# Who begins the first loads: two keys of the first step on ScalarE's queue, queries and a weight piece ahead of the next keys

## The chip, the cores and the metric

The kernel runs on one core of one Trainium2 chip. The metric is the device time of one execution in microseconds; lower is better.

## The reference

A delta-rule attention is followed by a two-layer network with a hard-swish.

```python
# q, k, v: (4, 8, 768, 48); beta: (4, 8, 768)
k_n = k / (np.linalg.norm(k, axis=-1, keepdims=True) + 1e-06)
for t in range(768):
    y[:, :, t] = einsum('bhd,bhde->bhe', q[:, :, t], state)
    v_old = einsum('bhde,bhd->bhe', state, k_n[:, :, t])
    state += beta[:, :, t] * outer(k_n[:, :, t], v[:, :, t] - v_old)
x = y.transpose(0, 2, 1, 3).reshape(3072, 384)
h = x @ w_in                       # (384, 2048)
g = h * clip(h + 3, 0, 6) / 6
out = g @ w_out                    # (2048, 384)
```

q, k, v and beta come as float32, the two weights as float64.

## The kernel before, in words

The 768 positions are taken in 24 steps of 32. In one step the 4 batches times 32 positions fill the 128 partitions, and the 8 heads lie side by side. A step t goes through these stages:

- `load_k` (L161) and `load_q` (L173) load its keys and queries, one DMA of 48 KB for each of the 4 batches, issued by SP (L168 and L180). `load_v` does the same for the values (L193).
- `norms` (L399): ScalarE squares the keys (L407), VectorE sums them (L413), ScalarE takes the root (L417), VectorE makes the inverse norm in four small instructions on the tiles `nt` and `inv` (L420, L422, L426, L431).
- `prep` (L505): GpSimd scales the keys into `kb` (L510); TensorE transposes keys and then queries (L524), and ScalarE copies each result out of PSUM into `KQ` (L532); TensorE forms the scores (L547), and VectorE masks them into `X` or `L` and `LB` (L558).
- The inverse of the lower triangle, for step 0 in `product` (L569): small products on TensorE (`pi`, L596) between VectorE transposes (L612, L626, L631 and so on) and copies by ScalarE (L624, L643). Steps 1 to 4 are inverted together by a chain on VectorE (`halves_of`), the later ones by fours.
- `chain` (state, output) on TensorE, and, two steps to a block, the two layers (`up`, `down` and their forms with fewer products), which are most of TensorE's time.

The weights arrive as float64 in 16 pieces of 768 KB, issued by SP in `load_w` (L331). Each is turned into float32 on the chip: four ScalarE activations over the piece (`scales`, L356), and three VectorE passes (`convert`, L378, L383, L389). The pieces w0 to w7 are of `w_in`. Beta comes in four loads of 24 KB, issued by ScalarE (`betas`, L1383), and is turned by VectorE (L255) into `beta_tok`. Constants are made in `settings`, among them `places` (L273), which the activations at L356 read. ScalarE's activation table is loaded at the head of the program (L201), followed by a copy of one column (L202).

The order of the opening is written out by hand in the string `ORDER`. Each word advances a generator by one step: `k` issues one of the 4 loads of a step's keys, `q` one of the queries, `w` one weight piece, `B` one beta load, `n0` one stage of the norms of step 0, `p0` one stage of its `prep`, `x0` one of its inverse, `a` one activation of `scales`, `c` one pass of `convert`, `z` and `s` settings, `m` masks. Every engine runs its own instructions in the order in which the words emit them.

The framework gives the loads of SP and ScalarE, in the order of the program, one of eight completion counters in turn. A load is held on its issuing engine until the load that had the same counter before it, eight loads earlier, has landed.

Of the kernel before, what the change touches and what calls it, by code (L numbers as in the profile page):

```python
# [19 lines left out]


ORDER = """
k*2 B*3 k*2 n0 k*2 z B s*2 n0*6 k*2 q*2 n1 q n1 q w k p0 z*3 k n1*2 k*2 n1*2 z p0*2 s k p0*3 a k a
m0 a n2 m1 p0 x0*2 w q x0 n1 x0*3 c*2 n2 a k s p1*2 a s*2 k q s*2 x0 n2 k*2 c x0 n2 x0 w q a*4 q p1
n2 k*2 a x0 m2 p1 c*2 p1 n2*3 b1 q b0 s p1 x0 q w x0 n2 q*2 c*3 x0 n4 k p1 k p2*2 x0*2 a*2 c a*2 q*3
a*2 w v p3*2 q x0 q n4 p2*2 c p2 v c n4*2 a*3 z v n4 c a m3 v c p2 n4*2 q p2 k c b2 h0 c h0 w a*2 h0
p4*2 a*2 m4 p3 q*4 h0 q k w p4*2 c*5 v*2 p3 k p3*3 k*2 p4*2 v*2 p4 m6 k a w a w i1*3 k i1*7 a i1*2 a
i1*2 v i1*2 k b3 k y0 c y0*3 ua*2 ra*2 i1*3 w v ga v a*3 i1*2 ua i1 h1 i1 q w ua ra ua i1 ra*2 ga i1
k ua a*2 ra ga i1 ga ua ra ua ra i1 ga i1*4 ua ga n5 x1*2 k x1 c a ra v a*2 ga x2 k*2 ga*2 ua*2 x1
ra*2 x1*2 ua h1*2 n5 k ga c ra ga*2 h1 c y1*2 ua ra w ga ua ra x2 n5 ga y1*2 ua ra ga h1 v*3 n5*2 k  # L30
y1*2 ua a ra x2 ub*2 a n5 rb*2 h1 x3 ga c*2 v W a h2 y2 gb ub rb gb x2 gb ub*2 n5*2 b4 rb n5 x2*2 h2
gb rb gb m5 a n5*2 ub rb gb v c q*2 v q*5 n5 ub n5 rb gb h2 y2 c h2 q ub y2*2 rb ub p5 b5 h2 rb gb*2
a*2 x3 p5 ub y2*2 k p5*2 h2 rb h3 p5 gb h3 ub*2 q rb gb rb gb ub a x3 p6 v c x4 x3 rb gb ub p7 rb gb
y3 c*2 v c p7*2 y3 v p7*2 b6 x3 q x3 ub h3 a p6*2 c p5*2 rb gb k m7 w p6 h3 u p6 k*2 q*3 a*2 y3 a p6
c y3 v y3*2 u n9 v k q a c a c*2 u*2 ru gu w k a*2 c a*2 x4 c*2 ru p7 a gu k u a*2 p7 p6 m8 u*3 a k
u*2 k h3 w ru*2 a*2 gu*2 x4 c*2 x4 k c*2 a p8 k a*2 u ru k h3 u*2 h4 ru a b8 gu k gu y4 p8*3 u h4
k*2 c q k*9 q u p8*2 k ru k*2 gu k c n9 q u q*2 p8 k*2 b7 n9*2 x4 i2 u x4 q i2*2 q ub ru gu u rb gb
i2*2 h4*2 u*2 i2 ru i2*6 y4 i2 gu i2*7 u i2 ru gu i2 u*3 ru i2*4 gu ru i2*2 v i2 c gu u*3 a u ru c
i2 u*2 i2 gu i2*3 q i2*5 y4 n9 i2 e*2 n9*2 i2*4 q i2 y4 e n9 u ru i2*3 u h4 i2 ru*2 gu h4 u n9 i2*2
u i2 e i2*6 y4 u k n9*3 u gu i2 y4 n9 i2 p9 q i2*2 gu  # L40
"""


# [1 line left out]
def kernel(  # L45
# [21 lines left out]
    nc = tc.nc  # L67
# [27 lines left out]
    def rows(b):  # L95
        return slice(C * b, C * b + C)
# [34 lines left out]
    def tokens(ap, b, t):  # L131
        return ap[b, :, t * C : (t + 1) * C, :].rearrange("h t d -> t h d")
# [25 lines left out]
            past.add(("read", key))  # L158
            reads.setdefault(key, len(reads))

    def load_k(t, eng=nc.sync):  # L161

        g, i = group(t)
        if g not in kfs:
            needs(*(("kb", first(g - 2) + j) for j in range(size(g - 2) if g >= 2 else 0)))
            kfs[g] = stage.tile([P, GS, H, D], FP32, name="kf", bufs=2)
        for b in range(B):
            eng.dma_start(out=kfs[g][rows(b), i], in_=tokens(k, b, t))  # L168
            if b == B - 1:
                past.add(("k", t))  # L170
            yield

    def load_q(t, eng=nc.sync):  # L173
        if t < N:
            if t >= NQB:
                needs(("qT", t - NQB))
            elif t:
                needs(*pad(t))
            for b in range(B):
                eng.dma_start(out=qbufs[t % NQB][rows(b), :, 0:D], in_=tokens(q, b, t))  # L180
                if b == B - 1:
                    past.add(("q", t))
                yield
# [14 lines left out]
    halves = const.tile([128, 2], FP32, name="halves")  # L198
    nc.vector.memset(halves[:], 0.5)
    half = halves[:, 1:2]  # L200
    nc.scalar.preload_act_table(ACTF.Sqrt)  # L201
    nc.scalar.activation(out=half, in_=halves[:, 0:1], func=ACTF.Copy)  # L202

    spare = const.tile([128, 3, NFC // 2 * DM // 2], FP32, name="spare")
    assert S <= spare.shape[2]
# [44 lines left out]
    def settings():  # L250

        nc.vector.memset(tiny, 1e-30)
        pads(nc.vector, kbufs[0], qbufs[0])
        yield
        nc.vector.transpose(out=beta_tok[:].rearrange("p n h -> p (n h)"), in_=beta_hm)  # L255
        past.add("beta")
        yield
        nc.vector.tensor_reduce(
            out=eye[:], in_=ident[:].rearrange("p (b c) -> p c b", b=B), axis=AX.X, op=ALU.add
        )  # L260
        nc.vector.tensor_reduce(
            out=blocks[:], in_=eye[:].rearrange("p (n c) -> p n c", c=G), axis=AX.X, op=ALU.add
        )
        past.add("blocks")
        yield
        nc.vector.tensor_reduce(
            out=corner[:], in_=ident[:].rearrange("p (b c) -> p c b", b=B)[:, C // 2 : C],
            axis=AX.X, op=ALU.add,
        )
        past.add("corner")  # L270
        yield
        for i, (_, _, value) in enumerate(powers):
            nc.vector.memset(places[:, i : i + 1], value)  # L273
        past.add("places")
        yield
        nc.vector.memset(parity[:], 0.0)
        for b in range(B):
            for j, value in enumerate((-1.0, 1.0)):
                nc.vector.memset(parity[rows(b), b % 2, j : j + 1], value)
        past.add("parity")  # L280
        yield
# [5 lines left out]
    def more_settings():  # L287
        for t in range(NBKB):
            pads(nc.gpsimd, bkbufs[t], *(x[t] for x in (kbufs, qbufs) if 0 < t < len(x)))
            past.add(f"pad{t}")  # L290
            yield
            if t == 1:
                nc.gpsimd.memset(state[:], 0.0)
                past.add(("state", -1))
                yield
# [49 lines left out]
    def scales():  # L345

        needs("places", "beta")
        for i in range(NW):
            if weights[i][1].dtype == FP32:
                continue  # L350
            if i >= 2:
                needs(("w", i - 2))
            needs(("raw", i))
            d, z = raws[i], like(es[i % 2], i)
            for n, (func, scale, _) in enumerate(powers):
                nc.scalar.activation(  # L356
                    out=z, in_=z if n else d.bitcast(I16)[:, :, :, 3], func=func,
                    bias=places[:, n : n + 1], scale=scale,
                )
                if n == 0:  # L360
                    past.add(("seen", i, 0))
                if n == len(powers) - 1:
                    past.add(("scale", i))
                yield
# [1001 lines left out]
    def pieces():  # L1366
        for i in range(NW):
            load_w(i)
            yield

    def queries():
        for t in range(N):
            for _ in load_q(t):
                yield

    def keys():
        for t in range(first(4) + GS):
            for _ in load_k(t):
                yield

    def betas():
        for b in range(B):
            nc.scalar.dma_start(out=beta_hm[C * b : C * b + H, :], in_=beta[b])  # L1383
            yield

    def values():
        for t in range(N):
            for _ in load_v(t):
                yield

    def early_norms(t):
# [4 lines left out]
    g_all = mlp.tile([128, NFC, TB], FP32, name="g", bufs=1)  # L1396
    rest = chained(convert(), quarters())
    gens.update(
        a=scales(), c=rest, w=pieces(), q=queries(), v=values(), B=betas(), k=keys(), z=settings(), s=more_settings(),
        ua=up(0, 0), ub=up(0, 1), u=mlp_units(),  # L1400
    )
    makers = {
# [4 lines left out]
    def behind_tensor(ins):  # L1407
        last = next(
            i for i in reversed(nc.cur_bb.bb.instructions) if i.engine == mybir.EngineType.PE
        )  # L1410
        tc.add_manual_dep(
            ins, last.name,
            mybir.DependencyInfo(mybir.DependencyClass.Sync, mybir.DependencyReason.DATA),
            reason="held back",
        )

    def do(word):
        if word in ("K", "Q", "V", "W"):
            n = len(nc.cur_bb.bb.instructions)
            next(gens[word.lower()])  # L1420
            (new,) = nc.cur_bb.bb.instructions[n:]
            behind_tensor(new)
        elif word in gens:
            next(gens[word])
        elif word[0] == "r":
            relus[word[1]].pop(0)()
        elif word[0] == "g":
            pending[word[1]].pop(0)()
        elif word == "e":
            evicts.pop(0)()  # L1430
        elif word[0] == "i":
            next(inverse_of(int(word[1:])), None)
        else:
            name, t = word[0], int(word[1:])
            if name == "p" and t >= LS + LE:
                next(prep_of(t), None)
            else:
                key = (name, t) if name in "hp" else ("early", name, t)
                next(made(key, lambda: makers[name](t)), None)
# [111 lines left out]
```

## Time and profile before

| | us |
|---|---|
| median of 3 runs | 667.3 |
| the runs | 667.3, 666.17, 667.43 |
| profiled execution | 665.93 |
| its span (first to last instruction) | 664.1 |
| TensorE matmul busy | 636.2 (96%) |
| VectorE busy | 487.1 (73%) |
| ScalarE busy | 272.1 (41%) |
| GpSimd busy | 203.5 (31%) |
| first key load issued (SP) | 0.80 |
| first Square on ScalarE (L407) | 4.78 |
| first weight piece issued (SP) | 6.75 |
| first L356 on ScalarE | 12.33 |

In the profile PE is TensorE, PEld its weight loads, DVE VectorE, ACT ScalarE, POOL GpSimd and SP SyncE; SPq and ACTq are issues of DMAs by the queues of SP and ScalarE. Line numbers are those of the kernel before; in the changed kernel the lines from L207 to L1383 stand five lower (L407 is L412), and the key loads are at L170. The granted clock is TensorE's, as a share of full speed.

### The profile page before, as it was taken

How to read it: one execution, taken by the hardware profiler on the slowest of the kernel's cores; microseconds unless marked ns; L12 is line 12 of the kernel's file. 1: busy time of each engine (PE TensorE's matmuls, PEld its weight loads, DVE VectorE, ACT ScalarE, POOL GpSimd, SP SyncE). 2: the span in 40 equal slices, each digit the busy share in tenths (PEclk: the TensorE clock that was granted, in tenths of full speed). 3: DMA queues.
4: the chain of work that ended last, by engine and by line, in shares of the span. 5: the costliest groups of instructions: out<-in, count | busy, mean ns of one | idle time of the engine just before them, and what ended most of it. 6: DMA issues, size and time to landing. Idle time of an engine off the chain costs nothing.

```text
span 664.1 us, 26330 instructions
## 1 busy us (share of the span) xinstructions
PE 636.2 (96%) x11544; PEld 568.1 (86%) x11544; DVE 487.1 (73%) x1146; ACT 272.1 (41%) x532; POOL 203.5 (31%) x320
## 2 busy tenths in 40 slices
PE   2769999999999999999999999999999999999997
PEld 1658987776789989989989999999999999999997
DVE  4899867898555697657979748989658998456353
ACT  5897679331233143142144244244244144153350
POOL 6531112003511320562254354064052241331430
PEclk9659999999999999999999999999999999999999
DMA  7897246212140030041030030020020020000000
GB/s 175 206 236 197 76 98 161 49 28 41 23 83 8 10 66 3 2 85 27 2 74 3 2 74 3 3 61 2 3 50 2 2 50 1 23 19 2 25 1 25
DMA packets 88499, 33.27 MB, mean 50 GB/s; under 512 B 80160, under 2 KB 83232, under 8 KB 88384
## 3 DMA queue, kind: packets, MB, share of 16 engines
q1 hardware_dynamic: 88128, 31.29, 20.9%
q8 instruction: 91, 1.49, 0.9%
q10 hardware_dynamic: 256, 0.30, 0.2%
q14 instruction: 24, 0.20, 0.1%
HBM read 26.84 MB, written 4.72 MB: 48 GB/s over the span
## 4 chain that ended last, share of the span: by engine, by line
PE 90%; DVE 3%; DMA 2%; SPq 2%; ACT 1%; issue 1%; POOL 0%; ACTq 0%; DVEq 0%; POOLq 0%
PE po L1218 28%; PE ph L1066 20%; PE ph L994 16%; PE po L1154 6%; PE ks L806 3%; PE pt L524 3%; PE su L938 3%; PE pz L827 3%; PE py L827 3%; PE sc L547 3%; PE yt L873 1%; DMA spare<-in_moe_w_in_dram 1%; PE pi L684 1%; DMA w_out<-in_moe_w_in_dram 1%; SPq L168 1%
## 5 line engine op out<-in xcount | busy, mean ns | idle before, releaser
L1066 PE MATMUL ph<-xT,w_in 128*128 128x128 f32 (+1 forms) x560 | 121.4, 321 | 0.7 <-ACT KQ L532 0.5
L994 PE MATMUL ph<-xT,w_in 128*128 128x256 f32 (+1 forms) x576 | 117.1, 353 | 0.9 <-ACT xT L877 0.6
L1218 PE MATMUL po<-w_out,g 128*128 128x192 f32 x640 | 110.6, 326 | 0.0
L994 PEld LDWEIGHTS ph<-xT,w_in 128*128 128x128 f32 x576 | 95.2, 194 | 13.9 <-ACT xT L877 1.0
L1218 PEld LDWEIGHTS po<-w_out,g 128*128 128x128 f32 x640 | 104.6, 190 | 0.5
L1066 PEld LDWEIGHTS ph<-xT,w_in 128*128 128x128 f32 x560 | 91.1, 191 | 5.9 <-ACT KQ L532 0.7
L1030 POOL TENSOR_TENSOR g<-g 128x256 f32<-128x256 f32 x112 | 67.9, 608 | 83.2 <-ACT g L1080 78.8
L1218 PE MATMUL po<-spare,g 128*128 128x192 f32 x480 | 86.7, 332 | 0.0
L1218 PEld LDWEIGHTS po<-spare,g 128*128 128x128 f32 x480 | 77.2, 190 | 1.8
L1001 ACT ACTIVATE g<-ph,halves 128x256 f32<-128x256 f32 (+1 forms) x96 | 41.0, 436 | 74.2 <-PE ph L994 74.2
L1228 POOL TENSOR_TENSOR o<-o,u 128x192 f32<-128x192 f32 x18 | 13.2, 731 | 175.8 <-ACT o L1225 97.2
L1080 ACT ACTIVATE g<-ph 128x512 f32<-128x512 f32 x56 | 33.4, 597 | 81.8 <-PE ph L1066 81.8
L1204 DVE TENSOR_TENSOR g<-g 128x512 f32<-128x512 f32 x80 | 55.5, 715 | 5.6 <-PE po L1218 5.6
L759 DVE TENSOR_TENSOR pr<-A 128x30 f32<-128x30 f32 (+9 forms) x150 | 57.5, 383 | 2.7
L764 DVE TENSOR_TENSOR A<-A,pr 128x30 f32<-128x30 f32 (+9 forms) x150 | 55.7, 371 | 3.7
L1004 DVE SCALAR_TENSOR_TENSOR g<-g,ph 128x256 f32<-128x256 f32 (+1 forms) x96 | 34.7, 371 | 29.4 <-ACT g L1001 29.0
L356 ACT ACTIVATE spare<-spare,places 128x768 uint16<-128x768 uint16 (+1 forms) x56 | 52.6, 944 | 2.8 <-DMA kf<-in_k_dram 1.7
L1093 DVE TENSOR_TENSOR g<-ph,g 128x256 f32<-128x256 f32 x56 | 23.5, 420 | 38.5 <-PE ph L1066 30.9
L1225 ACT ACTIVATE o<-po 128x192 f32<-128x192 f32 x40 | 13.2, 330 | 83.2 <-PE po L1218 79.6
L1154 PE MATMUL po<-w_out,g 128*128 128x384 f32 x128 | 45.2, 491 | 0.0
L1107 DVE SCALAR_TENSOR_TENSOR g<-o,g 128x512 f32<-128x512 f32 x56 | 40.7, 726 | 5.9 <-ACT o L1104 5.9
L1104 ACT ACTIVATE o<-g,halves 128x512 f32<-128x512 f32 x56 | 40.4, 722 | 8.7 <-DVE g L1107 5.7
(141 smaller groups left out, 989.1 us busy)
## 6 DMA issues: line engine op xcount, KB each, us to landing
kf<-in_k_dram SPq DMA_DIRECT2D x96, 48.0 KB, 2.4
qb<-in_q_dram SPq DMA_DIRECT2D x96, 48.0 KB, 2.8
vf<-in_v_dram SPq DMA_DIRECT2D x96, 48.0 KB, 2.2
out_dram<-o SPq DMA_DIRECT2D x92, 48.0 KB, 1.6
spare<-in_moe_w_in_dram SPq DMA_DIRECT2D x4, 768.0 KB, 5.9
w_out<-in_moe_w_in_dram SPq DMA_DIRECT2D x4, 768.0 KB, 6.0
w_out<-in_moe_w_out_dram SPq DMA_DIRECT2D x4, 768.0 KB, 6.9
spare<-in_moe_w_out_dram SPq DMA_DIRECT2D x4, 768.0 KB, 5.0
```

The costliest lines, as they stand in the source:

```text
L356: nc.scalar.activation(out=z, in_=z if n else d.bitcast(I16)[:, :, :, 3], func=func, bias=places[:, n : n + 1], scale=scale,)
L759: nc.vector.tensor_tensor(out=pv, in0=A[:, j + 1 :, j].unsqueeze(2).to_broadcast([n, w, j]), in1=A[:, j, 0:j].unsqueeze(1).to_broadcast([n ...
L764: nc.vector.tensor_tensor(out=A[:, j + 1 :, 0:j], in0=A[:, j + 1 :, 0:j], in1=pv, op=ALU.subtract)
L994: nc.tensor.matmul(ph[:, cols], lhsT=w_in[:, s, f * 128 : (f + 1) * 128], rhs=xT[:, s, cols], start=(s == 0), stop=(s == NKT - 1),)
L1001: nc.scalar.activation(out=g, in_=ph, func=ACTF.Relu, bias=half, scale=1.0 / 6.0)
L1030: nc.gpsimd.tensor_tensor(out=out, in0=a, in1=b, op=op)
L1066: nc.tensor.matmul(ph[:, n], lhsT=w, rhs=x, start=start, stop=stop, skip_group_check=True)
L1104: nc.scalar.activation(out=r, in_=g, func=ACTF.Relu, bias=half, scale=1.0 / 6.0)
L1107: nc.vector.scalar_tensor_tensor(out=g, in0=r, scalar=1.0, in1=g, op0=ALU.min, op1=ALU.mult)
L1154: nc.tensor.matmul(pos[c][:], lhsT=gs[blk, f // 2][:, f % 2, c * P : (c + 1) * P], rhs=w_out[:, f, :], start=(f == 0), stop=(f == NFC - 1),)
L1204: nc.vector.tensor_tensor(out=A(f, *out, 4), in0=A(f, *a, 4), in1=A(f, *b, 4), op=op)
L1218: nc.tensor.matmul(ps[n][:], lhsT=A(f - f % 2, *a)[:, f % 2], rhs=b[:, f], start=(f == 0), stop=(f == HF - 1),)
```

## The change

`load_k` and `load_q` issue from the engine in `issuer[0]`, which is SP. Two new words, `kA` and `qA`, set it to ScalarE for one load; only `kA` is used, twice, for the first two loads of step 0's keys. The table load and the copy behind it become a generator, `t`, and stand behind these two issues. In `ORDER` the opening words change as follows, up to `m1`; all words behind it are as they were.

- Step 0's four queries are issued right behind its keys, then the first weight piece, and only then step 1's four keys, which were ahead of the queries.
- The four beta loads stand two ahead of the first Square, one behind it and one behind step 0's root; they were three ahead and one behind the Square.
- On ScalarE, the first activation of w0 (`a`) now stands between the key copy and the query copy of step 0 (L532); the Square and the root of step 1, which were ahead of both copies, now follow the second. The other two of the first three activations stand behind that root.
- On VectorE, step 1's reduction and small norm instructions stand behind the turn of beta and the constants instead of among them, still ahead of step 0's X (L558).
- TensorE and GpSimd have the same instructions in the same order.

```diff
 ORDER = """
-k*2 B*3 k*2 n0 k*2 z B s*2 n0*6 k*2 q*2 n1 q n1 q w k p0 z*3 k n1*2 k*2 n1*2 z p0*2 s k p0*3 a k a
-m0 a n2 m1 p0 x0*2 w q x0 n1 x0*3 c*2 n2 a k s p1*2 a s*2 k q s*2 x0 n2 k*2 c x0 n2 x0 w q a*4 q p1
...
+kA*2 k*2 t q*4 B*2 n0 w B z n0*2 B s*2 n0*4 k*4 p0 z*3 p0*2 z p0 a p0*2 n1*2 s k*3 m0 n1*2 a k*2
+n1*2 a k m1 n2 p0 x0*2 w q x0 n1 x0*3 c*2 n2 a k s p1*2 a s*2 k q s*2 x0 n2 k*2 c x0 n2 x0 w q a*4 q
...
+    issuer = [nc.sync]
+
-    def load_k(t, eng=nc.sync):
+    def load_k(t):
...
-            eng.dma_start(out=kfs[g][rows(b), i], in_=tokens(k, b, t))
+            issuer[0].dma_start(out=kfs[g][rows(b), i], in_=tokens(k, b, t))
...
-    def load_q(t, eng=nc.sync):
+    def load_q(t):
...
-                eng.dma_start(out=qbufs[t % NQB][rows(b), :, 0:D], in_=tokens(q, b, t))
+                issuer[0].dma_start(out=qbufs[t % NQB][rows(b), :, 0:D], in_=tokens(q, b, t))
...
-    nc.scalar.preload_act_table(ACTF.Sqrt)
-    nc.scalar.activation(out=half, in_=halves[:, 0:1], func=ACTF.Copy)
+
+    def tables():
+        nc.scalar.preload_act_table(ACTF.Sqrt)
+        nc.scalar.activation(out=half, in_=halves[:, 0:1], func=ACTF.Copy)
+        yield
...
-        a=scales(), c=rest, w=pieces(), q=queries(), v=values(), B=betas(), k=keys(), z=settings(), s=more_settings(),
+        a=scales(), c=rest, w=pieces(), q=queries(), v=values(), B=betas(), t=tables(), k=keys(), z=settings(), s=more_settings(),
...
+        elif word in ("kA", "qA"):
+            issuer[0] = nc.scalar
+            next(gens[word[0]])
+            issuer[0] = nc.sync
```

More of the change, by code (lines that the diff above doesn't have):

```diff
@@ L22 @@
 ORDER = """
-k*2 B*3 k*2 n0 k*2 z B s*2 n0*6 k*2 q*2 n1 q n1 q w k p0 z*3 k n1*2 k*2 n1*2 z p0*2 s k p0*3 a k a
-m0 a n2 m1 p0 x0*2 w q x0 n1 x0*3 c*2 n2 a k s p1*2 a s*2 k q s*2 x0 n2 k*2 c x0 n2 x0 w q a*4 q p1
-n2 k*2 a x0 m2 p1 c*2 p1 n2*3 b1 q b0 s p1 x0 q w x0 n2 q*2 c*3 x0 n4 k p1 k p2*2 x0*2 a*2 c a*2 q*3
-a*2 w v p3*2 q x0 q n4 p2*2 c p2 v c n4*2 a*3 z v n4 c a m3 v c p2 n4*2 q p2 k c b2 h0 c h0 w a*2 h0
-p4*2 a*2 m4 p3 q*4 h0 q k w p4*2 c*5 v*2 p3 k p3*3 k*2 p4*2 v*2 p4 m6 k a w a w i1*3 k i1*7 a i1*2 a
@@ L28 @@
[L28 to L37, printed above, removed]
@@ L38 @@
-i2*2 h4*2 u*2 i2 ru i2*6 y4 i2 gu i2*7 u i2 ru gu i2 u*3 ru i2*4 gu ru i2*2 v i2 c gu u*3 a u ru c
-i2 u*2 i2 gu i2*3 q i2*5 y4 n9 i2 e*2 n9*2 i2*4 q i2 y4 e n9 u ru i2*3 u h4 i2 ru*2 gu h4 u n9 i2*2
-u i2 e i2*6 y4 u k n9*3 u gu i2 y4 n9 i2 p9 q i2*2 gu
+kA*2 k*2 t q*4 B*2 n0 w B z n0*2 B s*2 n0*4 k*4 p0 z*3 p0*2 z p0 a p0*2 n1*2 s k*3 m0 n1*2 a k*2
+n1*2 a k m1 n2 p0 x0*2 w q x0 n1 x0*3 c*2 n2 a k s p1*2 a s*2 k q s*2 x0 n2 k*2 c x0 n2 x0 w q a*4 q
+p1 n2 k*2 a x0 m2 p1 c*2 p1 n2*3 b1 q b0 s p1 x0 q w x0 n2 q*2 c*3 x0 n4 k p1 k p2*2 x0*2 a*2 c a*2
@@ new lines @@
+q*3 a*2 w v p3*2 q x0 q n4 p2*2 c p2 v c n4*2 a*3 z v n4 c a m3 v c p2 n4*2 q p2 k c b2 h0 c h0 w
+a*2 h0 p4*2 a*2 m4 p3 q*4 h0 q k w p4*2 c*5 v*2 p3 k p3*3 k*2 p4*2 v*2 p4 m6 k a w a w i1*3 k i1*7 a
+i1*2 a i1*2 v i1*2 k b3 k y0 c y0*3 ua*2 ra*2 i1*3 w v ga v a*3 i1*2 ua i1 h1 i1 q w ua ra ua i1
+ra*2 ga i1 k ua a*2 ra ga i1 ga ua ra ua ra i1 ga i1*4 ua ga n5 x1*2 k x1 c a ra v a*2 ga x2 k*2
+ga*2 ua*2 x1 ra*2 x1*2 ua h1*2 n5 k ga c ra ga*2 h1 c y1*2 ua ra w ga ua ra x2 n5 ga y1*2 ua ra ga
+h1 v*3 n5*2 k y1*2 ua a ra x2 ub*2 a n5 rb*2 h1 x3 ga c*2 v W a h2 y2 gb ub rb gb x2 gb ub*2 n5*2 b4
@@ new lines @@
+rb n5 x2*2 h2 gb rb gb m5 a n5*2 ub rb gb v c q*2 v q*5 n5 ub n5 rb gb h2 y2 c h2 q ub y2*2 rb ub p5
+b5 h2 rb gb*2 a*2 x3 p5 ub y2*2 k p5*2 h2 rb h3 p5 gb h3 ub*2 q rb gb rb gb ub a x3 p6 v c x4 x3 rb
+gb ub p7 rb gb y3 c*2 v c p7*2 y3 v p7*2 b6 x3 q x3 ub h3 a p6*2 c p5*2 rb gb k m7 w p6 h3 u p6 k*2
+q*3 a*2 y3 a p6 c y3 v y3*2 u n9 v k q a c a c*2 u*2 ru gu w k a*2 c a*2 x4 c*2 ru p7 a gu k u a*2
+p7 p6 m8 u*3 a k u*2 k h3 w ru*2 a*2 gu*2 x4 c*2 x4 k c*2 a p8 k a*2 u ru k h3 u*2 h4 ru a b8 gu k
@@ L41 @@
+gu y4 p8*3 u h4 k*2 c q k*9 q u p8*2 k ru k*2 gu k c n9 q u q*2 p8 k*2 b7 n9*2 x4 i2 u x4 q i2*2 q
+ub ru gu u rb gb i2*2 h4*2 u*2 i2 ru i2*6 y4 i2 gu i2*7 u i2 ru gu i2 u*3 ru i2*4 gu ru i2*2 v i2 c
+gu u*3 a u ru c i2 u*2 i2 gu i2*3 q i2*5 y4 n9 i2 e*2 n9*2 i2*4 q i2 y4 e n9 u ru i2*3 u h4 i2 ru*2
+gu h4 u n9 i2*2 u i2 e i2*6 y4 u k n9*3 u gu i2 y4 n9 i2 p9 q i2*2 gu
 """
```

## The prediction

> **What bounds the kernel now.** I read the page first, then the waits of the first 48 us, then the timeline of the first 45 us, then a table of stretches cut where the granted clock changes.
>
> ```profile
> span 664.1 us, 26330 instructions
> ...
> PE 90%; DVE 3%; DMA 2%; SPq 2%; ACT 1%; issue 1%; POOL 0%; ACTq 0%; DVEq 0%; POOLq 0%
> ```
>
> TensorE carries the chain. The change touches the first 16 us alone, in which the stretches (columns: stretch, then for each engine busy us and instructions, granted clock, DMA share, GB/s) show it mostly idle:
>
> ```profile
> 0.00:15.25 15.25, 3.91 (x136) 3.16 (x136) 7.34 (x29) 7.18 (x12) 8.81 (x36) 1.00 0.76 177
> 15.25:28.91 13.66, 10.05 (x332) 8.41 (x332) 11.35 (x20) 12.37 (x19) 7.00 (x12) 0.50 0.87 192
> 28.91:32.32 3.41, 1.69 (x71) 1.40 (x71) 3.09 (x8) 2.77 (x4) 2.29 (x3) 1.00 1.06 276
> 32.32:52.80 20.48, 15.13 (x417) 12.97 (x416) 19.07 (x49) 15.57 (x22) 6.09 (x9) 0.50 0.93 239
> ...
> 60.30:664.10 603.80, 599.08 (x10487) 536.34 (x10487) 439.00 (x1019) 226.91 (x464) 179.33 (x262) 1.00 0.16 34
> ```
>
> After 60.3 us TensorE is busy for 599.08 of 603.80 us, on work that the change leaves alone. So what it is worth is by how much the opening work reaches TensorE sooner. The waits before 48 us name two on loads (a third, GpSimd's `kb` at 26.09, follows the inverse norm that ended at 25.87):
>
> ```profile
> ACT sq L407 <- DMA kf<-in_k_dram: 2.7, 2, 2.5
> ...
> ACT spare L356 <- DMA kf<-in_k_dram: 1.7, 1, 1.7
> ```
>
> The timeline places them (start, duration, engine, line; count behind x):
>
> ```profile
> 0.80 3.82 SPq L168 DMA_DIRECT2D kf<-in_k_dram  x8
> ...
> 4.67 2.04 SPq L180 DMA_DIRECT2D qb<-in_q_dram  x4
> 4.78 0.52 ACT L407 ACTIVATE sq<-kf 128x384 f32<-128x384 f32 x1 [2.48 <-DMA kf<-in_k_dram]
> ...
> 6.75 0.45 SPq L331 DMA_DIRECT2D spare<-in_moe_w_in_dram  x1
> ...
> 10.07 0.60 ACT L532 ACTIVATE KQ<-pt 128x512 f32<-128x512 f32 x1 [0.26 <-PE pt L524]
> 10.24 0.45 SPq L331 DMA_DIRECT2D spare<-in_moe_w_in_dram  x1
> ...
> 12.02 0.43 DVE L558 TENSOR_TENSOR X<-sc,sums_in 128x256 f32<-128x256 f32 x1 [2.10 <-PE sc L547]
> ...
> 12.27 0.31 SPq L180 DMA_DIRECT2D qb<-in_q_dram  x1
> 12.33 2.92 ACT L356 ACTIVATE spare<-spare,places 128x768 uint16<-128x768 int16 x3 [1.66 <-DMA kf<-in_k_dram]
> ...
> 15.56 0.36 ACT L624 ACTIVATE sums_in<-pi 128x256 f32<-128x256 f32 x1
> ...
> 15.96 0.45 DVE L626 STREAM_TRANSPOSE sums_in<-pi 128x256 f32<-128x256 f32 x1 [1.62 <-ACT sums_in L624]
> ```
>
> L356 waits on several loads, and the view names a key; but SP's own stall ends at 12.27, at a load that by its place waits for weight piece w0 (issued 6.75). So w0 lands at 12.25, 5.5 us after its issue. Three L356 (2.92 us) and a Square (15.15) then hold ScalarE, though the products that L624 reads ended at 14.39 (13.64 + 0.75). L624 at 15.56 releases VectorE at 15.96, which is nearly full from there (19.07 of 20.48 us in the fourth stretch). Hence my measure: **when L624 starts**. From there on every engine has the same instructions in the same order in both kernels, and no row from 13 to 48 us waits for a load in fact.
>
> **The change, part by part.**
> *First keys.* Two of four loads go from SP to ScalarE. SP's eight first issues take 3.82 us, 0.49 apart; on ScalarE two beta issues stand 0.62 apart (1.79 and 2.41). The last of the four is now issued at 0.81 + 0.62 = 1.43 rather than 2.20. The four landed 1.8 to 2.5 us after issue; with 2.1 the last is there at 3.55 instead of 4.67. Behind the two issues come the table load (1.28 us, 0.81 before) and a small copy (0.20): 1.75 to 3.25, under the landing. Without that cover they cost at most 1.5 us. Square goes from 4.78 to 3.65, by 1.1 us, and so do the chain to `kb` (7.18, now 6.05; GpSimd is free from 5.29) and the key transposes.
> *Queries.* The four issues go from 4.67 to 1.71; landing 2.2 us later they are long there when TensorE asks (about 7.9). They bound nothing before either: no cost, no gain of their own.
> *Weight piece w0.* A load waits for the eighth before it, as eight completion counters go round. The fourth query waits for ScalarE's second key (3.45), and w0 stands behind it: 3.95. With the 5.5 us of its row it lands at 9.45, 2.8 us sooner; with 4.6, the fastest weight piece of the trace, at 8.55; with the fourth query at 3.9, at 9.9.
> *But ScalarE's order changes.* The first L356 now stands between the two KQ copies of step 0. It waits for w0 (9.5), takes 0.95, and the second KQ copy runs at 10.45, where it was at 10.07. So the 1.1 us won on the keys is gone: queued behind that wait are the query copy, TensorE's scores L547 and VectorE's X L558.
> *Step 1's keys behind w0.* They were issued before w0 and squared at 6.42. Now they queue behind it: the six keys behind w0 before took 4.5 to 5.1 us where two first ones took 2.1. The fifth of the six, issued at 9.26 with 4.5, was there 1.5 us behind w0, so the fourth is some 1.3 behind it: 10.75. Square runs behind the KQ copy at 10.9. VectorE has step 1's reduction, reciprocal and two products ahead of X L558 in both kernels; they were done by 9.9, two us before X. Square of step 0 to the end of that chain took 4.78 to 6.87, so 10.9 + 2.1 = 13.0: X goes from 12.02 to 13.0, one us late. X to the end of the products is 14.39 − 12.02 = 2.37, so L624 starts at 15.4. ScalarE is free by then: root at 12.0, two L356 to 14.2, the next Square to 14.7.
> *Sum.* 15.4 − 15.56 = −0.15 us; with w0 at 8.55 it is bounded by ScalarE at 14.7, −0.85; with w0 at 9.9, +0.3.
> *Betas.* The last is issued behind the first root, 4.8 as before; the turn of beta on VectorE (7.44) and `places` (9.83 to 10.2) end by 9.0, ahead of w0. If beta lands one us late in the weight traffic, L356 starts 0.5 late.
> *GpSimd* has no new order. Its second `kb` waits for an inverse norm behind X: 14.42 becomes 15.4. TensorE transposes it at 18.32 after other products, and GpSimd idles 6.2 us from 19.9, so this is hidden.
> *SP, and the second weight piece w1.* The fifth key behind w0 is now the eighth load after it and waits for its landing: 9.45, then four issues of 0.49, and w1 at 11.4 instead of 10.24. A piece issued after a like stall (26.45) was there at 31.6, in 5.15 us, so w1 lands at 16.55 instead of 16.1. ScalarE's fifth L356 wants it at 16.7. Later pieces hang on it through the same counters, 0.4 late: the sixth was there at 37.5 (SP's stall ends) and is read at 37.99, 0.5 us of cover. So nothing is lost as long as w1 slips by no more than 0.5.
>
> The profiled run took 665.93 us (1.8 around its span); less 0.15 that is 665.8. The median shown is 667.3, 1.4 above it, and 666.17 is among its runs; I forecast **667.1** as a median. A measurement of this kernel can tell about 0.2% (1.33 us) from no change: below 665.97 is faster, above 668.63 slower. The own range of this case is the sum's −0.85 to +0.3 and the spread of the runs shown: 665.9 to 667.7.
>
> **Rivals.**
> *A, w0 early.* Keys and w0 land at their fastest, L624 follows ScalarE at 14.7: −0.85, 666.4; with a run as low as 666.17 that is faster. For it: DMA is busy only 0.42 in the first 5 us. Against it: the 5.5 was taken in the same company of loads.
> *B, the clock falls otherwise.* Four transposes L524 took 1.11 us at 40.29, granted 0.50, and 0.66 at 31.68, granted 1.00. Twelve on the chain at 40.3 to 43.1, at full clock, save 3 × 0.45 = 1.35; with the state products L938 (1.27 against 0.82 at 68.19) 1.8. That gives some 665.6: faster. The stretches show grants of 3.41 us and its multiples, and TensorE is a little more or less dense when the opening moves. Against it: TensorE's order is the same, and the grant can as well be lost at 28.91 to 32.32, for +0.5. [...]
> *C, slower: w1 comes late.* Its place is SP's queue behind the fifth key. Weight pieces took 4.6 to 6.9 us; with 6.9 w1 lands at 18.3, 2.2 late, and beyond the cover of 0.5 that lands on ScalarE at the sixth piece: +1.7, 668.8. It decides for slower from a slip of 1.8. Against it: the 6.9 were taken with much queued ahead, and here the queue has just run dry.
> *D, the change doesn't do what it says.* The keys land no sooner, at 4.7, since the DMA engines and not the issue set their pace. Then w0, whose counter waits for a first key, goes out at 4.75, lands at 10.25, and L624 starts at 16.2: +0.7, 667.9. For it: landings trailed issues by more and more, 1.8 to 2.5. Against it: the DMA share of 0.42. [...]
>
> **How the numbers follow.** Forecast 0.44, A 0.12, B 0.18, C 0.14, D 0.12. Faster is B with the lower edge of A and of the forecast: 0.18 + 0.05 + 0.03 = 0.26. Slower is C with the upper edge of D and of the forecast: 0.14 + 0.03 + 0.02 = 0.19. The rest, 0.55, is the same. The range takes in B's 665.6 with a little below, and D and most of C: 665.3 to 668.7.
>
> **What would show it.** In the changed profile: first Square at 3.6 to 3.7; SP's first weight issue near 4, its stall ending near 9.4; the second KQ copy behind an L356 (now L361), near 10.4; X (L563) near 13.0 and behind a `nt` product; the L624 copy (now L629) near 15.4; w1 issued near 11.4. I am wrong if X starts near 12 (then step 1's keys were early), if L629 is more than 0.9 away from 15.4, if a row after 16 us waits for a weight piece, or if the granted clock changes at other places between 28 and 53 us and TensorE's chain with it.

## The result, and the profile after

The changed kernel takes 669.69 us in the median (668.46 to 671.16), the kernel before in the same session 666.06 (665.24 to 667.43): a ratio of 1.0054 with an interval of 1.0037 to 1.007, that is 3.6 us slower. The profiled execution took 669.25 us, its span is 667.4. The lines of the page that answer to the span and the chain of before, and the line of the queue that matters below (it is the same in both):

```profile
span 667.4 us, 26328 instructions
...
PE 634.3 (95%) x11544; PEld 566.4 (85%) x11544; DVE 486.6 (73%) x1146; ACT 273.2 (41%) x532; POOL 204.6 (31%) x320
...
q8 instruction: 91, 1.49, 0.9%
...
PE 90%; DVE 3%; DMA 2%; ACT 2%; issue 2%; SPq 1%; POOL 0%; ACTq 0%; DVEq 0%; POOLq 0%
```

On the chain ScalarE and "issue" went from 1 to 2% each. The table of stretches, cut where the granted clock changes, says how far the loss reaches:

```profile
31.36:34.77 3.41, 1.85 (x72) 1.62 (x72) 3.08 (x9) 2.42 (x4) 2.64 (x3) 1.00 0.60 139
34.77:48.42 13.65, 8.48 (x274) 7.12 (x274) 11.20 (x29) 11.26 (x16) 3.45 (x4) 0.50 0.92 222
...
63.75:667.40 603.65, 598.46 (x10487) 536.28 (x10487) 439.84 (x1022) 228.21 (x465) 179.64 (x262) 1.00 0.15 33
```

The last stretch holds the last 10487 products in both kernels. The first of them starts at 64.55 instead of 60.29, 4.26 us later, and from there to the end of the span it is 602.85 us where it was 603.81. So the whole loss lies in the opening, and some 1 us of it comes back later. The clock isn't what made it slower: half speed was granted for 13.65 us here and for 34.1 us before.

The timeline shows the first loss:

```profile
3.69 0.45 SPq L336 DMA_DIRECT2D spare<-in_moe_w_in_dram  x1
4.01 0.52 ACT L412 ACTIVATE sq<-kf 128x384 f32<-128x384 f32 x1 [0.75 <-DMA kf<-in_k_dram]
...
5.16 0.28 ACTq L1388 DMA_DIRECT2D spare<-in_beta_dram  x1
...
10.16 0.98 DVE L260 STREAM_TRANSPOSE beta_tok<-spare 128x768 f32<-128x768 f32 x1 [3.83 <-DMA kf<-in_k_dram]
...
11.73 0.08 DVE L278 MEMSET places<- 128x1 f32 x4
...
11.82 0.98 ACT L361 ACTIVATE spare<-spare,places 128x768 uint16<-128x768 int16 x1 [2.77 <-DVE places L278]
...
12.71 0.57 ACT L537 ACTIVATE KQ<-pt 128x512 f32<-128x512 f32 x1
...
15.19 0.42 DVE L563 TENSOR_TENSOR X<-sc,sums_in 128x256 f32<-128x256 f32 x1
...
17.95 0.38 ACT L629 ACTIVATE sums_in<-pi 128x256 f32<-128x256 f32 x1 [1.11 <-PE pi L601]
```

Before, the last beta load and its turn stood here:

```profile
4.80 0.28 ACTq L1383 DMA_DIRECT2D spare<-in_beta_dram  x1
...
7.44 0.97 DVE L255 STREAM_TRANSPOSE beta_tok<-spare 128x768 f32<-128x768 f32 x1
```

Square is early, 4.01 instead of 4.78. The last beta load is issued 1.5 us behind w0 and lands at 9.96, 4.8 us after its issue; before it took 1.7 us (4.80 to 6.53). The beta load ahead of it, issued 0.34 us behind w0 (4.03), took 3.8 us and landed at 7.83. VectorE's turn of beta waits for the last one, to 10.16 instead of 7.44 (the row names a key load that has the same completion counter). L361 needs that turn twice over: `places` is set behind it on VectorE, and L361 writes over the raw betas (its scratch and the betas' landing place are the same part of `spare`). ScalarE therefore stands at 11.82 with w0 long there (9.29), and behind L361 stand the query copy and step 1's Square. X comes at 15.19 and L629 at 17.95, 2.39 us later than before.

The second loss is on TensorE, in its own rows of the timeline:

```profile
35.58 1.16 PE L552 MATMUL sc<-KQ 64*32 64x64 f32 x62 [0.69 <-ACT KQ L537]
39.03 0.37 PE L552 MATMUL sc<-KQ 64*32 64x64 f32 x2 [2.29 <-issue]
...
43.61 0.45 PE L943 MATMUL su<-R,sums_in 32*64 32x48 f32 x3 [0.89 <-issue]
...
49.83 0.35 PE L552 MATMUL sc<-KQ 64*32 64x64 f32 x16 [0.69 <-issue]
```

The same products before:

```profile
33.78 1.18 PE L547 MATMUL sc<-KQ 64*32 64x64 f32 x64 [0.69 <-ACT KQ L532]
...
39.91 0.45 PE L938 MATMUL su<-R,sums_in 32*64 32x48 f32 x3 [0.50 <-issue]
...
43.80 2.10 PE L547 MATMUL sc<-KQ 64*32 64x64 f32 x128 [0.69 <-ACT KQ L532]
```

TensorE stops 2.29 us between two products of one loop with nothing to wait for that the view can name, again for 0.89 us, and for 0.69 at 49.83. Before there was one such stop in the opening, of 0.50 us ahead of the last three of L938. The trace has a queue for it: q8 moves 91 packets of 16 KB, and TensorE has 2 x 11544 instructions, 254 to a packet. So q8 seems to bring TensorE's instructions in blocks of 127 pairs of weight load and product, and 2 + 64 (L832) + 61 = 127 pairs lie between the first two stops. The ends of its packets bear this out. In the changed kernel packets end at 37.48, 42.07 and 48.52, and TensorE starts again 1.55, 1.54 and 1.31 us later. At all 40 such stops of 0.25 us and more before 75 us, in the 13 profiles of this case that have any, it starts again 1.25 to 1.79 us behind the end of a packet.

The packet that belongs to the first stop started at 32.21 before, with w5 issued at 32.37. In the changed kernel w5 is issued at 31.18, the product one block earlier starts 2.1 us later (33.17 instead of 31.06), and the packet starts at 36.00 and takes 1.48 us instead of 1.02.

How the stops reach the end can be followed on VectorE. Its masks of the scores, before and then after:

```profile
29.21 0.41 DVE L558 TENSOR_TENSOR L<-sc,mb 128x256 f32<-128x256 f32 x1
...
36.59 0.38 DVE L558 TENSOR_TENSOR L<-sc,sums_in 128x256 f32<-128x256 f32 x1
...
46.01 0.42 DVE L558 TENSOR_TENSOR L<-sc,sums_in 128x256 f32<-128x256 f32 x1 [0.17 <-PE sc L547]
...
60.29 0.73 PE L684 MATMUL pi<-X,sums_in 16*32 16x16 f32 x64 [1.01 <-DVE sums_in L694]
```

```profile
31.31 0.41 DVE L563 TENSOR_TENSOR L<-sc,mb 128x256 f32<-128x256 f32 x1
...
39.51 0.42 DVE L563 TENSOR_TENSOR L<-sc,sums_in 128x256 f32<-128x256 f32 x1 [0.74 <-PE sc L552]
...
50.35 0.42 DVE L563 TENSOR_TENSOR L<-sc,sums_in 128x256 f32<-128x256 f32 x1 [0.82 <-PE sc L552]
...
64.55 0.73 PE L689 MATMUL pi<-X,sums_in 16*32 16x16 f32 x64 [0.92 <-DVE sums_in L699]
```

VectorE is 2.10 us late ahead of the stops, 2.92 behind the first and 4.34 behind the third. From there its chain of the inverse runs without a wait to TensorE's products at 64.55, 4.26 us late.

### The profile page after: what moved, and what is told of

It reads as the page before. It is cut to its first block, busy times and chain, and to the rows that moved or that the text cites. A ratio compares the mean times of both kernels' runs of the same rounds, so it can differ in the third digit from the quotient of the medians.

```text
span 667.4 us, 26328 instructions
## 1 busy us (share of the span) xinstructions
PE 634.3 (95%) x11544; PEld 566.4 (85%) x11544; DVE 486.6 (73%) x1146; ACT 273.2 (41%) x532; POOL 204.6 (31%) x320
## 3 DMA queue, kind: packets, MB, share of 16 engines
q1 hardware_dynamic: 87584, 31.19, 20.8%
## 4 chain that ended last, share of the span: by engine, by line
PE 90%; DVE 3%; DMA 2%; ACT 2%; issue 2%; SPq 1%; POOL 0%; ACTq 0%; DVEq 0%; POOLq 0%
PE po L1223 28%; PE ph L1071 20%; PE ph L999 15%; PE po L1159 6%; PE ks L811 3%; PE pt L529 3%; PE pz L832 3%; PE su L943 3%; PE py L832 3%; PE sc L552 3%; PE yt L878 1%; PE pi L689 1%; DMA spare<-in_beta_dram 1%; DMA kf<-in_k_dram 1%; ACT spare L361 1%
## 5 line engine op out<-in xcount | busy, mean ns | idle before, releaser
L999 PE MATMUL ph<-xT,w_in 128*128 128x256 f32 (+1 forms) x576 | 115.6, 350 | 2.4 <-DVE g L1009 1.8
L361 ACT ACTIVATE spare<-spare,places 128x768 uint16<-128x768 uint16 (+1 forms) x56 | 52.6, 944 | 3.9 <-DVE places L278 2.8
```

The lines of the kernel that those rows point to most:

```text
L361: nc.scalar.activation(out=z, in_=z if n else d.bitcast(I16)[:, :, :, 3], func=func, bias=places[:, n : n + 1], scale=scale,)
L999: nc.tensor.matmul(ph[:, cols], lhsT=w_in[:, s, f * 128 : (f + 1) * 128], rhs=xT[:, s, cols], start=(s == 0), stop=(s == NKT - 1),)
```

## The experiments

All times beside the kernel before on the same chip; the ratio is this run's time over that of the kernel before, with its 95% interval. "L629" is the start of step 0's copy, 15.56 before.

| run | L629 | ratio |
|---|---|---|
| the change | 17.95 | 1.0054 (1.0037 to 1.007) |
| betas_first | 17.38 | 1.0048 (1.0022 to 1.0073) |
| a_behind | 17.56 | 1.0054 (1.0029 to 1.0079) |
| w0_behind_keys | 17.48 | 1.0058 (1.004 to 1.0075) |
| w5_later | 17.77 | 1.0045 (1.0024 to 1.0067) |
| keys_queries | 17.04 | 1.0054 (1.0036 to 1.0072) |
| beta_aside | 15.92 | 1.0014 (0.9992 to 1.0035) |
| keys_only | 14.60 | 0.998 (0.9958 to 1.0001) |
| keys_again | 14.64 | 0.9974 (0.9952 to 0.9995) |
| keys_copy | 14.26 | 0.9975 (0.9955 to 0.9996) |

### betas_first: the four betas ahead of the first Square

```diff
-kA*2 k*2 t q*4 B*2 n0 w B z n0*2 B s*2 n0*4 k*4 p0
+kA*2 k*2 t q*4 B*4 n0 w z n0*2 s*2 n0*4 k*4 p0
```

> The changed kernel with all four beta loads ahead of the first Square on ScalarE. Beta theory (the last beta load, issued at 5.16 with w0 in flight, comes only with w0 and holds the turn of beta, L361 and the query copy): the last beta is issued near 4.3, lands near 7.9, the turn of beta starts near 8.0 instead of 10.16, L361 near 9.7 instead of 11.82, L629 near 15.8 instead of 17.95; the time falls by 2 us or more, to some 666.5 to 667.5. Rival, step 1's keys behind w0: they still come at 10.7, and the time stays within 1 us of 669.7. Rival, ScalarE's issues: the Square starts later still (4.5), and the time stays or rises.

A miss. The last beta waited for its completion counter until 4.51, still behind w0 (3.68), and the turn of beta ran at 9.60, not 8.0; X at 14.62. Issued 0.65 us sooner, it took as long as in the change, 4.9 us (4.8 there): its place on ScalarE was not what held it. The held issue also kept Square to 4.89 (4.01 in the change), as the last rival had it, but that decided nothing: the query copy stood behind L361 (11.26) as before.

### keys_only and keys_again: step 0's two keys on ScalarE, everything else as before

```diff
-k*2 B*3 k*2 n0 k*2 z B s*2 n0*6
+kA*2 t B*3 k*2 n0 k*2 z B s*2 n0*6
```

> The kernel before with only this done: two of step 0's key loads issued by ScalarE, its table load behind them. Beta theory: the betas stay ahead of w0, so nothing is lost; 665.5 to 666.5, no difference that can be told. Rival, step 1's keys behind w0: the same, since they stay ahead of it. Rival, ScalarE's issues and the later table load cost the time: 668 or more.

Square at 4.23, w0 issued at 6.04, behind all betas (the last at 4.26), the turn of beta at 6.89, L629 at 14.60. This part of the change is good by itself. It was run again with the last group:

> The run that moved step 0's two keys alone, once more, beside the others of this call: the ratio was 0.998 with an interval that just touches 1. Theory T: L629 near 14.6, ratio 0.997 to 0.9995. Rival: no difference, 0.9995 to 1.001.

L629 at 14.64, and this time the interval ends just below 1. The two measurements agree on 0.20 and 0.26% less than the kernel before: a gain, at the edge of what these runs can tell. Of the edits tried, this one and keys_copy, which is built on it, are the only ones that came out below the kernel before.

### a_behind: the first L361 behind the query copy

```diff
-z p0 a p0*2 n1*2
+z p0*3 a n1*2
```

> The changed kernel with the first L361 behind step 0's query copy and scores instead of ahead of the copy. The beta theory has two ways to X: through L361 and the query copy, and through GpSimd's masks L491, which need the turned beta and end near 12.4. With the first way opened the query copy runs near 9.3, and X starts near 12.9 instead of 15.19, held by the mask and step 1's chain; the time falls by some 2 us to 667.5 to 668. If the order on ScalarE matters little, X stays at 15 and the time at 669.7. Rival, step 1's keys: Square of step 1 then starts at 10.7 when its keys land, X at 12.9 also, so this kernel does not tell the two apart, but it tells both from the rival of ScalarE's issues, which expects no gain.

A miss that taught the order. The query copy ran at 9.47, yet X only at 14.80: step 1's Square stayed queued behind L361 on ScalarE (11.93, Square at 12.81), and VectorE has step 1's chain ahead of X. Two things stood behind the held L361, and freeing one gave 0.4 us at L629.

### w5_later: the sixth weight piece behind four queries

```diff
-c h0 w a*2 h0 p4*2 a*2 m4 p3 q*4 h0
+c h0 q*4 w a*2 h0 p4*2 a*2 m4 p3 h0
```

> The changed kernel with the sixth weight piece issued behind four query loads that followed it on SP. In the changed kernel TensorE stands still from 36.7 to 39.0 in the middle of L552, and a 16 KB instruction fetch, which started at 36.0 where the same point of the order was 34.3, runs in that time. Theory: the fetch queues behind the sixth piece's data; with the piece issued 2 us later the fetch starts near 34.3, the standstill goes, and 1.5 us of the 3.6 go with it: 668.2. Rival, the standstill has another cause or is made up for later: it stays, or the time stays within 0.5 of 669.7. The start of L629 is 17.95 by both.

Ratio 1.0045 (1.0024 to 1.0067): the expected gain of 1.5 us can't be told from none. The first stop was gone: its packet started at 34.83, with w5 issued at 34.30 instead of 31.18, and took 0.88 us. But TensorE stood 1.84 us at L943 (44.49) and 1.84 at L552 (51.92). The packet for L943 started 3.8 us behind the product one block earlier (41.64 behind 37.87; 1.4 us in the change), while w5 and the next piece had been issued at 34.30 and 36.72 (31.18 and 35.33 there). So an early w5 made the first stop, and putting it off only moved the stopping; what held the later packets was not traced.

### beta_aside: the betas land elsewhere, `places` set ahead of their turn

```diff
-    beta_hm = spare[:, 2, 0:S]
+    beta_hm = spare[:, 2, S : 2 * S]
...
         nc.vector.memset(tiny, 1e-30)
+        for i, (_, _, value) in enumerate(powers):
+            nc.vector.memset(places[:, i : i + 1], value)
```

> The changed kernel with two edits that take away what holds the first L361: the raw betas land in the other half of the third part of `spare`, so that L361 no longer overwrites what VectorE's turn of beta still has to read, and the memset of `places` stands ahead of the turn of beta. Theory T (betas that complete only with w0 hold VectorE's turn, and with it L361, the query copy and step 1's Square): the betas still land near 10, but L361 starts with w0, near 9.4, the query copy near 10.3, step 1's Square near 11.1 (its keys land at 11.04), X near 13.0 to 13.4, L629 near 15.4 to 15.8, as the prediction had them; compute is back in time against the weight loads, TensorE's standstills of 2.29, 0.89 and 0.69 us in L552 and L943 go, and the time is 666 to 667.5, about that of the kernel before. Rival R1 (the order of the loads alone does it, by what the early weights do to the traffic): X and L629 come back, but TensorE still stands still near 37 us, and the time is 668.5 to 670.

The loads and their order are those of the change; what held L361 is gone. Its timeline:

```profile
9.15 0.97 ACT L361 ACTIVATE spare<-spare,places 128x768 uint16<-128x768 int16 x1
...
9.82 0.98 DVE L262 STREAM_TRANSPOSE beta_tok<-spare 128x768 f32<-128x768 f32 x1 [3.51 <-DMA kf<-in_k_dram]
...
10.03 0.58 ACT L537 ACTIVATE KQ<-pt 128x512 f32<-128x512 f32 x1
...
13.17 0.41 DVE L563 TENSOR_TENSOR X<-sc,sums_in 128x256 f32<-128x256 f32 x1
...
15.92 0.38 ACT L629 ACTIVATE sums_in<-pi 128x256 f32<-128x256 f32 x1 [1.45 <-PE pi L601]
```

The betas are nearly as late as in the change (9.82 for their turn, 10.16 there), and L361 no longer waits for them: it starts with w0 (9.12). X is at 13.17 and L629 at 15.92, nearly what the prediction had (13.0 and 15.4), and the kernel is level with the one before. So the held L361 is the first loss. Of the second, 2.1 us in L552 (0.70 and 1.37) and 0.6 in L943 are still there in this profile: the forecast that the stops would go was too bold.

### w0_behind_keys: w0 behind step 1's keys, ScalarE's order as changed

```diff
-kA*2 k*2 t q*4 B*2 n0 w B z n0*2 B s*2 n0*4 k*4 p0
+kA*2 k*2 t k*4 q*4 B*2 n0 w B z n0*2 B s*2 n0*4 p0
```

> The changed kernel with step 1's four keys issued ahead of the queries and w0, as they were; ScalarE's order stays that of the change, the first L361 between the two KQ copies. Betas then land before w0, the turn of beta runs near 7 and `places` near 9.3. Theory T with two causes (late betas, and an L361 that stands ahead of the query copy whatever it waits for): L361 now waits for w0 itself, landing near 11.4, the query copy runs near 12.3, X near 14.7, L629 near 17.1; TensorE's fetch comes late and stands still as in the changed kernel; time 668.5 to 670. Rival R2 (the betas alone do it, the place of L361 is harmless): X near 12, L629 near 15, time 665.5 to 667.

As expected of two causes, the order of the loads and the place of L361: w0 went out at 5.85, behind the last beta (5.12; 5.16 in the change, where w0 was ahead), the turn of beta ran at 7.62 instead of 10.16, and L361 then waited for w0 itself, to 11.37; query copy 12.24, X 14.71. An L361 ahead of the query copy costs two us whichever of its inputs is late. The change fails from both ends: with w0 early the betas are late, with w0 late L361 is.

### keys_queries: two of step 0's queries issued by ScalarE too

```diff
-kA*2 t B*3 k*2 n0 k*2 z B s*2 n0*6 k*2 q*2 n1 q n1 q w k
+kA*2 t B*3 k*2 n0 k*2 z B s*2 n0*6 k*2 qA*2 n1 q n1 q w k
```

> The kernel before with step 0's first two keys and first two queries issued by ScalarE, the table load behind the two keys, w0 in its old place behind the queries; a try at a version that beats both. SP's w0 issue comes two issues (0.98 us) sooner than in the run that moved the keys alone (6.04 there): near 5.1, landing near 10.5, while the betas, all issued by 4.3, land before it. Theory T: L361 starts near 10.6 instead of 11.36, L629 near 13.9 instead of 14.60, no standstill of TensorE; time 665 to 666, 0.5 to 1 us less than with the keys alone. Rival R3 (ScalarE's two more issues sit ahead of step 1's Square and delay VectorE's chain or the betas): X later than 11.6, time 666 to 667.5.

A miss, and a second case of the same kind. SP was free sooner, so w0 went out at 5.08, and ScalarE's two query loads 0.3 us behind it:

```profile
5.08 0.39 SPq L336 DMA_DIRECT2D spare<-in_moe_w_in_dram  x1
5.34 0.84 ACTq L182 DMA_DIRECT2D qb<-in_q_dram  x2
...
11.21 1.09 PE L529 MATMUL pt<-ident,qb 128*128 128x128 f32 x4 [2.60 <-DMA qb<-in_q_dram]
```

w0 landed at 10.61, the queries at 10.91 and 11.11, and TensorE waited 2.60 us for them. X was at 14.27. The betas, all ahead of w0, were in time (the last at 6.86): late betas aren't needed for a loss of this kind, another small load behind w0 brings it too.

### late_copy: the loads of before, L624 made eight times

```diff
-        nc.scalar.activation(out=V, in_=ps[:, 0, :], func=ACTF.Copy)
+        for _ in range(8):
+            nc.scalar.activation(out=V, in_=ps[:, 0, :], func=ACTF.Copy)
```

> The kernel before, its loads and their order untouched; the copy L624 of step 0 is made eight times instead of once, which delays VectorE from L626 on by some 2.0 us (7 times 0.27, the spacing of that row to the next). Theory T (the second loss is TensorE's own instruction fetch, which comes 2 us later against weight loads that do not move, and queues behind w5): TensorE stands still by 1 to 2.5 us near 36 to 39 us and again before 55, as in the changed kernel, and the time is 3 to 4 us above the kernel before, 669 to 670.5. Rival R1 (the standstills come from the changed order of loads): no standstill beyond the 0.5 of the kernel before, the delay is partly taken back, and the time is 1 to 2 us above, 667 to 668.3.

The copies took 3.27 us, so L626 (L627 here) came 2.88 us late, not 2.0. The ratio is 1.0045 (1.0026 to 1.0064), 3.0 us (1.7 to 4.3): by the time alone either theory could hold. TensorE's rows decide:

```profile
39.87 0.37 PE L547 MATMUL sc<-KQ 64*32 64x64 f32 x2 [1.68 <-issue]
...
44.71 0.45 PE L939 MATMUL su<-R,sums_in 32*64 32x48 f32 x3 [1.17 <-issue]
...
52.03 0.47 PE L547 MATMUL sc<-KQ 64*32 64x64 f32 x16 [1.59 <-issue]
```

The stops are at the same three products as in the changed kernel, with the loads in the order of before. So compute that is late against the weight loads is enough for them, and a changed order of the loads isn't needed. (In this profile half speed was granted from 15.25 to 59.62 us, so its end can't be set against the others.)

### fetch_shift and half_block: TensorE's instructions moved against their blocks

```diff
+            for i in range(32 if t == 0 and j == 1 else 0):
+                nc.tensor.matmul(
+                    pt[rows(i % 4), i // 4 % 4, 0:32], lhsT=ident[0:64, 0:32], rhs=ident[0:64, 0:32],
+                    start=True, stop=True,
+                )
             for p in range(NP):
                 nc.tensor.transpose(
```

Above is half_block; fetch_shift had 64 products, all into one corner of `pt`.

> The changed kernel with 64 small products of TensorE added ahead of step 0's query transposes, into the PSUM tile that these then overwrite; TensorE is idle there (the transposes end at 9.27, the copy that reads them starts at 12.71), so they cost nothing by themselves. They shift every later block of 256 instructions (128 pairs of weight load and product), which is what one instruction fetch of 16 KB brings, by half a block. Theory T (the standstills called issue are waits for instruction fetches): L629 stays near 17.95, and the standstills move to 64 pairs earlier in TensorE's order: the 2.29 us ahead of the last two products of L552 near 39 and the 0.89 ahead of the last three of L943 near 43.6 are gone from there, and appear ahead of or at the start of that L552 group and near the end of L832's 64 products. How much time that saves depends on what TensorE waits for there anyway: between nothing and 2 us, 667.5 to 670. Rival R4 (something else in TensorE's queue, a wait on PSUM or a semaphore at those products): the standstills stay at the same products.

The dose was wrong twice. Each of these float32 products is two pairs in the trace (128 for the 64), so they make a whole block, and a shift by a block leaves the stops where they are (1.14 us ahead of the last two of L552, 0.32 ahead of the last three of L943). q8 had 92 packets instead of 91. And into one corner the pairs took 55 ns each, 7.03 us together, which was not hidden: ratio 1.0091 (1.0058 to 1.0123). Its profile shows a granted clock of 0.565, so only the places are read from it.

> The changed kernel with 32 small products ahead of step 0's query transposes. In the run with 64 of them the trace counts 128 pairs of weight load and product, one whole block of 256 instructions, and the standstills stayed ahead of the last two products of L552 and the last three of L943, as a period of one block would have it; that told nothing apart. 32 are 64 pairs, half a block. Theory T (waits for instruction fetches): the two standstills leave these products and come 64 pairs earlier in TensorE's order: at the end of the query transposes ahead of that L552 group, and ahead of the last two or so of L832's 64 products; L629 near 17.95; time 667.5 to 670.5. Rival R4 (a wait that belongs to those products): 1 to 2.5 us still stand ahead of the last two of L552 and 0.5 to 1 ahead of the last three of L943.

The 64 pairs took 1.08 us in idle time, and L629 was at 18.12. TensorE's rows (lines five lower again):

```profile
36.44 1.18 PE L557 MATMUL sc<-KQ 64*32 64x64 f32 x64 [0.69 <-ACT KQ L542]
37.55 1.50 PE L837 MATMUL pz<-vf,X 32*32 32x48 f32 x62
40.23 0.36 PE L837 MATMUL pz<-vf,X 32*32 32x48 f32 x2 [1.18 <-issue]
...
47.86 0.71 PE L837 MATMUL py<-R,LB 32*32 32x48 f32 x48
54.00 0.55 PE L837 MATMUL py<-R,LB 32*32 32x48 f32 x16 [5.43 <-issue]
```

The stops left L552 (here L557) and L943 (L948) and stand ahead of the last two of `pz` and, 64 pairs behind the old place of the third stop (112 of L552's 128), ahead of the last 16 of `py`. The second (L943) has none 64 pairs on. So they belong to the block of instructions, not to the products. Where the expectation erred is the price: one stop became 5.43 us, its packet starting at 51.34, with two pieces of `moe_w_out` issued between 46 and 54, five more stops of 0.17 to 1.85 us came between 74 and 109 us, and the ratio rose to 1.0141 (1.0089 to 1.0194), for 1 us of work in idle time.

### keys_copy: the keys alone, and L629 ahead of the third L361

```diff
-a m0 a n2 m1 p0 x0*2 w q x0 n1 x0*3
+a m0 m1 p0 x0*2 w q x0 n1 x0 a n2 x0*2
```

> The run that moved step 0's two keys alone (ratio 0.998), with one more step on ScalarE: the third L361 of w0 and the Square behind it stand behind L629 instead of ahead of it. There L629 ran at 14.60 right behind that Square, while X to the end of its products takes 2.37 (11.46 to 13.83). Theory T (what the opening gives L629 early is kept or grows): L629 near 13.9, no standstill of TensorE, 664.5 to 665.8, ratio 0.996 to 0.998. Rival R5 (VectorE is the bound from 16 us on, its next pass waits for the Square or the fourth scale): no gain over the keys alone, 665.7 to 666.5.

L629 at 14.26, not 13.9, and no gain over keys_again. Stops of 1.3 us at L943 and 0.5 at L832 are in this profile. 0.4 us more at L629 can't be told from none.

## Why the prediction was wrong, by its own steps

- *First keys.* Right in kind, too large: Square went from 4.78 to 4.01, not 3.65; the last key was counted as landed at 3.94, not 3.55. keys_only, where this step stands alone, agrees: the last key was issued 0.95 us sooner than before, and Square came 0.55 sooner, at 4.23.
- *Queries and w0.* w0 was issued at 3.69 (forecast 3.95) and landed at 9.29 (9.45). One detail was wrong: by the turn of the counters, which goes across both queues, w0 had to wait for SP's second key (landed at 3.62), and the query ahead of it for SP's first (2.76), not for ScalarE's second (3.94).
- ***Betas*: the step that failed.** The turn of beta and `places` were to "end by 9.0, ahead of w0. If beta lands one us late in the weight traffic, L356 starts 0.5 late." They ended at 11.14 (10.16 + 0.98) and at 11.82. The price was that of a beta with no weight piece in flight; with one it took 4.8 us, and what waits behind L361 was charged for 0.5 us of it and not for the 2.5 from w0's landing (9.29) to L361 (11.82). From this term come the query copy at 12.71 (10.45), X at 15.19 (13.0) and L629 at 17.95 (15.4). beta_aside, with that term taken out, gives 10.03, 13.17 and 15.92.
- *Step 1's keys.* The chain ahead of X was named rightly, Square, sum, root and products, but it hung on L361 as the query copy did (a_behind). The keys themselves were there at 10.37 (10.75) and held nothing.
- *The measure.* "From there on every engine has the same instructions in the same order in both kernels", so L624's delay was to count one for one. This is the second step that failed. In the changed kernel 2.39 us at L629 were 2.10 on VectorE at 31 us, grew behind the three stops to 4.26 at TensorE (64.55), and were 3.4 from 128 us on and 3.1 at its last product. The table points the same way, with intervals of 1 to 1.7 us to either side: −0.96 at L629 gave 1.3 to 1.7 us less, +1.5 to +2.4 gave 3.0 to 3.9 more; late_copy is the exception, 2.88 gave 3.0. The loads didn't move with compute: w5 was issued 1.19 us sooner, while the mask at 31 us was 2.10 late. TensorE's instruction packets did, that of the first stop from 32.21 to 36.00, and so they started under other traffic. Where the last us was regained was not traced beyond this: it came back between 72 and 111 us, and 0.35 of it between 319 and 345.
- *SP and w1.* Right for w1: issued at 11.32 (11.4), landed at 16.41 (16.55). Wrong for the later pieces, which were to be 0.4 late: w2 to w5 were issued 0.3, 0.3, 0.9 and 1.2 us sooner than before. The danger was then not a late piece but an early one: w5 at 31.18 stood ahead of a packet of TensorE's instructions, and the first stop went when it was put off (w5_later).
- *The rivals.* A and D are out by the keys and w0 alone, C by w1's landing. B's clock was in fact kinder, 20 us less at half speed: the 18 products at 53.33 took 2.27 us at full clock, where they took 3.61 at half. But TensorE then waited 1.23 and 0.57 us for VectorE (59.17 and 60.68), so the gain was lost: TensorE was not the bound there. None of the rivals was what happened. Of the signs of being wrong, L629 was 2.55 us away from 15.4, and the clock changed at other places; a row after 16 us waited too, though for TensorE's own instructions and not for a weight piece.

That small loads issued behind w0 come late is shown by after, betas_first, beta_aside and keys_queries: the last beta landed 0.3 to 0.7 us behind w0, the two queries 0.3 and 0.5. It isn't strictly the order of issue: the beta issued 0.34 us behind w0 landed 1.5 us ahead of it. The packets in the trace say where the time went. The last beta's eight packets of 3 KB started at 7.64 to 8.73, 2.5 to 3.6 us after its issue, where they had started 0.9 to 1.1 us after it before (5.69 to 5.94); w0's 384 packets of 2 KB started between 4.82 and 8.33, from 7 us on mixed with those of the keys behind it. So the wait was mostly ahead of the packets. A smaller part was behind them: from the start of the last one to the last completion count took 1.23 us (8.73 to 9.96), before 0.59 (5.94 to 6.53); the last beta's final seven counts came between 9.50 and 9.96, w0's ended at 9.29. What orders the packets and the counts is open: no run here shows it.

## What to carry to other kernels

Before a large load is moved ahead, list each small load that will be issued behind it on any queue, price it at about the large load's landing (here between 1.5 us ahead of it and 0.7 behind), and follow who waits for it, through shared buffers too. An instruction moved up on its engine brings all its inputs' lateness to everything that the program queues behind it there (here L361, held to 11.82, took the query copy from 10.07 to 12.71). Where weights stream in, being late by 2 us can cost 3 or 4 (here 2.39 at L629 became 3.6), so a change that helps should be tried alone: the two keys on ScalarE, without the rest, were the gain.

## What was not expected of the hardware

TensorE's instructions come by DMA beside the data (in the changed kernel q8 takes 0.9% of the time of the 16 engines, q1, which carries most of the data, 20.8%): 16 KB for each 127 pairs, 0.9 to 1.8 us a packet in the first 75 us, with stops of 0.5 us in the kernel before, 2.29 in the changed one and 5.43 in half_block, in loops that have all their data. Between the first two stops of the changed kernel the trace has 127 pairs and two semaphore instructions of TensorE, 256 in all; over the whole kernel it has 23270 such records, 255.7 to a packet. Rows that wait for "issue" between two products of the same loop are where to see it. Thirty-two products in idle time, which did little but shift the blocks, moved the time by more (1.0141) than the change itself.
